# One more turn of queries in the wait for the fold: a recurrent attention's forward loop on one Trainium2 core

## The chip, the cores and the metric

The kernel runs on one core of a Trainium2 chip, as one launch. The metric is the device time of that launch in microseconds (us). The engines are named as the profile names them: PE (TensorE's matmuls), PEld (its weight loads), DVE (VectorE), ACT (ScalarE), POOL (GpSimd) and SP (SyncE, which only issues transfers here). PE reads its operands from SBUF and writes to PSUM; DVE and ACT copy from PSUM to SBUF.

## The reference, cut to what matters

The program is one training step, forward and all gradients, of `x + s * g`: `g` is a gated feed-forward of the normalised input, `s` a recurrent attention over it. Only the recurrence matters here:

```python
for s in range(n_seg):                       # 64 segments of 32 tokens
    h = concatenate([mem, xs], axis=1)       # 8 memory rows and 32 tokens, 640 wide
    q, k, v = h @ Wq, h @ Wk, h @ Wv         # 32 heads of 128
    p = softmax(where(mask, q k^T * scale, -1e9))
    o = (p v) @ Wo
    mem = o[:, :M]                           # the next segment's memory
    outs.append(o[:, M:])
```

Only the 8 memory rows pass from one segment to the next, so a segment's memory rows are a chain through all 64 steps. The tokens' rows of a segment hang on the chain, but nothing of the chain hangs on them.

## The kernel before, in words

`phase3_Afwd` (L389) runs the forward recurrence. Its loop, in `recurrence` (L555), has 64 steps. A step `t` consists of two things woven into each other:

- `chain(t, gap)` (L598): the memory rows of segment `t`. With `packed_half` (L301) it projects hx (8 memory rows and 24 riding rows, turned) by Wk, Wq and Wv, each in two halves, into the PSUM banks bA and bB. DVE copies the halves of Wk and Wq to SBUF (`k.copy`, L90), ACT those of Wv; `packed_sel` (L311) picks out the memory rows. Then come scores (L647), a soft-max over DVE and ACT, the weighted sum (L682), and the output projection `packed_out` (L317, matmuls at L325). `fold_add` (L330) then folds that projection's two halves: ACT copies one half (fup, L334), DVE adds the other in two parts (fsum, L336). `fold_turn` (L346, L352) turns the sum on PE, and DVE writes it into the next step's hx (L699). Nothing of step t + 1 can be projected before that.
- The batched work of the tokens of earlier segments, three segments together in a "tile" `tl`, in units of four heads `(tl, qd)`. A tile has eight units, three in two of the steps and two in the third (SPL, L890), from step 3 on (`batch`). `FILL` (L918) puts their parts into the gaps of the chain, which are named W0, W1, V0, W2, G1 to G6.

The parts of a unit that the change and the steps of the prediction touch:

- `ld("q", ...)` (L747): SP loads a unit's queries, memory rows (L245 or L754) and token rows (L265), into `xq`, of which there are two buffers. The first and second unit of step t + 1 are loaded in gap G1 of step t, the third in G5.
- `turn_q` (L760): four matmuls against the identity (L765) turn the four heads' queries into a PSUM tile qpt, and one ACT copy (L767) brings it to one of three SBUF tiles xqT. In before it is called for a step's first unit in G5 of the step ahead, for the second in W0, for the third in G1. `scores` (L769), which reads them, comes in G2.
- `turn_p` (L835): the same for the soft-max's results (L840, DVE copy L841); they come from POOL's `norm` (L832).
- `pv` (L882; matmuls L860 and L863), in W0 and W1, and `kprep` (L738, matmuls L743), in G4 and, for a third unit, in W0.
- The PSUM tiles of all of these come from one pool of five (tag "x"): a new one waits until an earlier one is read out.

At the end of some gaps PE gets filling matmuls without a use (L914, L915): the identity times 512 columns of Wq, into bank bA or bB. `WARM` (L564) says how many: one in G2, two in G3, two in G5. G5 lies between `fold_add` and `fold_turn`.

The order of all instructions is that of the program as written: `in_order` (L273, called at L1065) holds every engine to it. Semaphores alone decide when each one starts.

Of the kernel before, what the change touches and what calls it, by code (L numbers as in the profile page):

```python
# [554 lines left out]
def recurrence(k, W0, W4, Wv, Wk_, Wq, Wo, own, ps, banks):  # L555
    nc, tc = k.nc, k.tc
    D, DC, S, H, HD, T = k.D, k.DC, k.S, k.H, k.HD, k.T
    with tc.tile_pool(name="achain", bufs=1) as ch, \
# [5 lines left out]
        WARM = dict(G2=1, G3=2, G5=2)  # L564

        def ride_ld(t):
            x0 = k.NB0 + 24 * t
            b, sub = t // 4, t % 4
            if sub == 0 and x0 < S:
                w = min(96, S - x0)  # L570
                rt = ch.tile([P, DC, 96], BF16, name="ride", tag="ride")
                turned_load(k, rt[:, :, 0:w], k.XN[x0:x0 + w, :])
                rides[b] = (rt, w)
# [133 lines left out]
        def w_alloc(nm_):  # L707
            if nm_ == "o":
                WT["o"] = W0.tile([P, DC, HD], BF16, name="WoT", tag="w0")
                src = k.A_Wo.rearrange("h e d -> (h e) d")  # L710
                wfetch.extend([(WT["o"][:, :, r:r + 256], src[r:r + 256, :]) for r in range(0, HD, 256)])
            elif nm_ == "q":
                WT["q"] = W0.tile([P, H, D], BF16, name="WqT", tag="w1")
            else:
                WT["k"] = W4.tile([P, H, D], BF16, name="WkT", tag="w2")
                src = k.A_Wk.rearrange("d h e -> d (h e)")
                wfetch.extend([(WT["k"][:, h0:h0 + 2, :], src[:, h0 * P:(h0 + 2) * P]) for h0 in range(0, H, 2)])

        def w_ld(n):
            for _ in range(n):  # L720
                if wfetch:
                    turned_load(k, *wfetch.pop(0))
# [9 lines left out]
        def ld_k(tl, qd):  # L732
            c0 = qd * 512
            kr = fl.tile([96, 512], BF16, name="kr", tag="kr", bufs=2)
            k.load_x(kr, 0, k.x_src(tl, "k", c0, c0 + 512), nc.sync)
            uu["kr", tl, qd] = kr

        def kprep(tl, qd, eng='s'):  # L738
            ns, nm, nx, n = k.geo(tl)
            kr = uu.pop(("kr", tl, qd))  # L740
            pt = ps.tile([P, 4, nx], BF16, name="kpt", tag="x", bufs=5)
            for j in range(4):
                nc.tensor.transpose(pt[:, j, :], kr[0:nx, j * P:(j + 1) * P], k.ident[0:nx, 0:nx])  # L743
            dst = kTs[tl % 2][:, qd * 4:qd * 4 + 4, 0:n].rearrange("p h (s c) -> p h s c", c=40)[:, :, :, 8:40]
            k.copy(dst, pt[:].rearrange("p h (s c) -> p h s c", c=32), eng=eng)

        def ld(w, tl, qd, eng=nc.sync):  # L747
            nm = k.geo(tl)[1]
            c0 = qd * 512
            r = fl.tile([120, 512], BF16, name=f"x{w}", tag=f"x{w}", bufs=2 if w == "q" else 3)  # L750
            if qd >= (5 if w == "q" else 2):
                ns, nm, nx, n = k.geo(tl)
                g0 = 512 * (qd % 2)
                eng.dma_start(r[nx:n], k.QVM[3 * tl:3 * tl + ns, :, qd // 2, "qv".index(w), g0:g0 + 512].rearrange("t r c -> (t r) c"))  # L754
            else:
                k.load_m(r, tl, w, c0, c0 + 512, eng)
            k.load_x(r, 0, k.x_src(tl, w, c0, c0 + 512), eng)
            uu[w, tl, qd] = r
# [45 lines left out]
        def soft_exp(tl, qd, j0=0, j1=4):  # L804
            n = k.geo(tl)[3]
            sp, (nmx, Z), Pb = uu["s", tl, qd], uu["m", tl, qd], xPs[qd % 3]
            if nmx is None:
                nc.scalar.activation(Pb[0:n, :, 0:n], sp[0:n], ACT.Exp, scale=k.scale)
                uu["zs", tl, qd] = Pb
            else:  # L810
                for j in range(j0, j1):
                    nc.scalar.activation(Pb[0:n, j, 0:n], sp[0:n, j, :], ACT.Exp, bias=nmx[0:n, j:j + 1], scale=k.scale,  # L812
                                         accum_out=Z[0:n, j:j + 1])
            if j1 == 4:
                uu["z", tl, qd] = Z
                uu.pop(("s", tl, qd))
                uu.pop(("m", tl, qd))
# [25 lines left out]
        def oride_ld(t):  # L843
            if 0 <= t - k.OT0 < k.NO:
                r = ch.tile([P, H, 24], BF16, name="oride", tag="oride")
                nc.sync.dma_start(r[:], k.OTX[t - k.OT0])
                uu["o", t] = r

        def oride(t):
            if 0 <= t - k.OT0 < k.NO:  # L850
                nc.gpsimd.tensor_copy(oTm[:, :, 8:32], uu.pop(("o", t))[:])
# [15 lines left out]
        def pv_turned(tl, qd, eng='s', qo=nc.scalar):  # L867
            v, pt, po = uu["pv", tl, qd]
            if pt is not None:
                ot = fl.tile([P, 4, 4, 24], BF16, name="xoT", tag="xoT", bufs=2)  # L870
                k.copy(ot[:].rearrange("p c h t -> p h c t"), pt[:].rearrange("p h (c t) -> p h c t", t=24), eng=eng)
                qo.dma_start(k.OTX[4 * tl:4 * tl + 4, :, 4 * qd:4 * qd + 4, :].rearrange("c p h t -> p c (h t)"),
                             ot[:].rearrange("p c h t -> p c (h t)"))
# [17 lines left out]
        batch = {}  # L891
# [5 lines left out]
        def gap_of(t):  # L897
            def at(f, tt, i):
                b = batch.get(tt, ())
                if i < len(b):  # L900
                    f(*b[i])

            def gap(g):
                FILL(g, t, at, kbatch)
                if t == T - 1:
                    if g == "G1":
                        w_alloc("o")
                        ld("q", *tail[0])
                        ld("q", *tail[1])
                    if g == "G2":  # L910
                        next(work)
                    if g in ("G2", "G4"):
                        w_ld(2)
                for i in range(WARM.get(g, 0)):  # L914
                    nc.tensor.matmul((bA if g == "G4" else bB)[:], k.ident[:], Wq[:, 0, 0:512], start=True, stop=True)  # L915
            return gap

        def FILL(g, t, at, kbatch):  # L918
            kb = kbatch.get(t, ())
            if g == "W0":  # L920
                oride_ld(t)
                at(pv, t - 1, 0)
                at(turn_q, t, 1)
                for u in kbatch.get(t - 1, ())[2:]:
                    kprep(*u)
            elif g == "W1":
                at(pv_mm, t - 1, 1)
                at(pv_turned, t - 1, 1)
                at(turn_p, t - 1, 2)
                at(lambda a, b: ld("v", a, b), t - 1, 2)  # L930
            elif g == "V0":
                at(pv_rows, t - 1, 1)
            elif g == "W2":
                ride_ld(t + 1)
                for u in kb[0:2]:
                    ld_k(*u)
            elif g == "G1":
                oride(t)
                at(pv_mm, t - 1, 2)
                at(turn_q, t, 2)  # L940
                for i in range(2):
                    at(lambda a, b: ld("q", a, b), t + 1, i)
            elif g == "G2":
                at(lambda a, b: pv_turned(a, b, qo=nc.gpsimd), t - 1, 2)
                at(pv_rows, t - 1, 2)
                for i in range(3):
                    at(scores, t, i)
                at(soft_max, t, 0)
                for i in range(2):
                    at(lambda a, b: ld("v", a, b), t, i)  # L950
            elif g == "G3":
                at(lambda a, b: soft_exp(a, b, 0, 2), t, 0)
                at(soft_max, t, 1)
            elif g == "G4":
                at(lambda a, b: soft_exp(a, b, 2, 4), t, 0)
                at(lambda a, b: soft_max(a, b, True), t, 2)
                at(norm, t, 0)
                at(soft_sub, t, 2)
                for u in kb[0:2]:
                    kprep(*u, 'v')  # L960
                for u in kb[2:]:
                    ld_k(*u)
                at(soft_exp, t, 1)
                at(norm, t, 1)
                at(soft_exp, t, 2)
            elif g == "G5":
                at(turn_p, t, 0)
                at(turn_q, t + 1, 0)
                at(lambda a, b: ld("q", a, b), t + 1, 2)
            elif g == "G6":  # L970
                at(turn_p, t, 1)
                at(norm, t, 2)
# [56 lines left out]
        batch = {t: b for t, b in batch.items() if t < T}  # L1029
# [1262 lines left out]
```

## Time and profile before

| | us |
|---|---|
| Median of three runs | 4702.92 (4698.06 to 4706.8) |
| The profiled execution | 4684.61 |
| Its span, first to last instruction | 4682.7 |
| PE busy | 4466.5 (95%) |
| PEld busy | 2821.1 (60%) |
| DVE busy | 2244.7 (48%) |
| POOL busy | 2098.4 (45%) |
| ACT busy | 1587.4 (34%) |
| Mean granted clock of PE | 0.988 of full |
| L915, the fillers: 320 matmuls, one each | 0.379 |
| L765, turns of queries: 704 matmuls, one each (median) | 0.216 |
| L767, their ACT copies: 176, one each (median) | 0.558 |

The forward loop lies between about 369 and 1582 us of the span. Matmuls run into each other in PE's pipeline, and their ends are modelled, so the duration of one is longer than the distance to the next; costs of PE are better read from the starts. Weight loads (PEld) run beside matmuls. The releaser in brackets behind a row is what ended the idle time of its engine just before it.

### The profile page before, as it was taken

The page shows a single profiled execution, that of the slowest core. Times are in us where ns is not written, and L with a number is a line of the kernel's source. Part 1 is how long each engine was busy: PE and PEld are TensorE (multiplying, and loading weights), DVE is VectorE, ACT ScalarE, POOL GpSimd, SP SyncE. Part 2 cuts the span into 40 slices and gives each one's busy share as a digit, 9 for nine tenths or more (in the row PEclk, how much of TensorE's full clock was granted, in tenths as well). Part 3 has the DMA queues.
Part 4 walks back from the last instruction along what each step waited for, and adds up shares of the span by engine and source line. Part 5 has one row for each costly group of instructions (what it writes and reads, how often), then busy time and mean ns, then how long its engine had stood idle before and what let it go on. Part 6 is the DMA issues. An engine that isn't in the chain of part 4 may idle for free. (4 is left out here: it accounts for less than half of the span.)

```text
span 4682.7 us, 159785 instructions
## 1 busy us (share of the span) xinstructions
PE 4466.5 (95%) x64504; PEld 2821.1 (60%) x64504; DVE 2244.7 (48%) x7156; ACT 1587.4 (34%) x4360; POOL 2098.4 (45%) x3528
## 2 busy tenths in 40 slices
PE   8999999999999898999999998999999999999999
PEld 4544555555555555666666665676667666666675
DVE  8734666666666534555555553343224432311460
ACT  5432555555544433333333332232223322200000
POOL 6532555555555423455444444354335533311440
PEclk9999999999999998999999999999999999999999
DMA  8773566666655677777777775664345543579783
GB/s 269 236 252 119 175 178 178 179 179 179 180 168 167 167 181 230 211 225 207 215 211 209 208 209 154 144 163 132 110 116 158 147 129 107 170 223 207 159 181 100
DMA packets 976843, 834.77 MB, mean 178 GB/s; under 512 B 518890, under 2 KB 858286, under 8 KB 974144
## 3 DMA queue, kind: packets, MB, share of 16 engines
q1 hardware_dynamic: 763879, 547.92, 42.2%
q0 software_dynamic: 129952, 228.13, 16.4%
q10 hardware_dynamic: 82275, 48.52, 4.0%
q8 instruction: 509, 8.34, 0.8%
q14 instruction: 228, 1.87, 0.1%
HBM read 472.66 MB, written 310.33 MB: 167 GB/s over the span
## 5 line engine op out<-in xcount | busy, mean ns | idle before, releaser
L1667 PE MATMUL wg<-gr,hr 128*128 128x512 bf16 x2400 | 521.7, 379 | 0.0
L1648 PE MATMUL g<-land,ghacc 128*128 128x320 bf16 x3072 | 459.9, 300 | 0.8
L1667 PEld LDWEIGHTS <-hr 128*128 128x128 bf16 x2400 | 233.9, 98 | 278.9
L306 PEld LDWEIGHTS <-hx 128*32 128x32 bf16 x10240 | 246.8, 96 | 229.1 <-issue 14.6
L1648 PEld LDWEIGHTS <-ghacc 128*128 128x128 bf16 x3072 | 289.2, 98 | 104.2 <-ACT ghacc L92 2.2
L90 DVE CAST wgo<-wg 128x512 bf16<-128x512 f32 x72 | 49.8, 692 | 471.2 <-PE wg L1667 471.2
L90 DVE CAST stg<-bank 128x512 bf16<-128x512 f32 x256 | 177.1, 692 | 158.6 <-PE bank L306 154.5
L880 POOL DMA_DIRECT2D OR<-xv x163 | 89.8, 551 | 361.1 <-ACT xv L92 338.5
L1613 POOL DMA_DIRECT2D GSP<-grs x48 | 25.5, 542 | 473.1 <-ACT grs L1605 472.0
L92 ACT COPY ghacc<-t6g 128x768 bf16<-128x768 bf16 (+1 forms) x176 | 137.1, 779 | 293.8 <-PE t6g L1630 284.5
L1324 POOL DMA_DIRECT2D VTD<-gvT x176 | 129.4, 742 | 218.7 <-ACT gvT L1323 209.5
L325 PEld LDWEIGHTS <-gkv 128*8 128x8 bf16 x8192 | 177.6, 86 | 82.2 <-issue 4.1
L832 POOL TENSOR_TENSOR xP<-xP,xrz 120x480 bf16<-120x480 bf16 x163 | 161.1, 988 | 76.0 <-DVE xrz L831 46.6
L812 ACT ACTIVATE xP<-xsp,xnm 120x120 bf16<-120x120 f32 (+1 forms) x540 | 186.1, 372 | 26.0 <-DVE xnm L794 25.9
L1654 DVE TENSOR_TENSOR ghacc<-ghacc,g 128x320 f32<-128x320 f32 x192 | 93.6, 487 | 209.9 <-PE g L1648 209.9
L336 DVE TENSOR_TENSOR fsum<-bank,fup 64x160 bf16<-64x160 f32 x254 | 69.5, 311 | 258.5 <-ACT fup L334 255.2
L92 ACT CAST wgo<-wg 128x512 bf16<-128x512 f32 x48 | 28.1, 585 | 479.8 <-PE wg L1667 407.0
L1371 POOL DMA_DIRECT2D GXP<-gks x157 | 91.0, 580 | 189.5 <-ACT gks L1369 188.8
L325 PE MATMUL bank<-Wo,oTm 128*32 128x320 bf16 x4032 | 154.2, 307 | 18.4 <-DVE oTm L684 18.4
L325 PE MATMUL bank<-WkT,gkv 128*8 128x320 bf16 x4096 | 162.8, 299 | 4.2 <-issue 2.2
L325 PE MATMUL bank<-WvT,gkv 128*8 128x320 bf16 x4096 | 166.4, 305 | 0.5 <-DVE gkv L1197 0.5
L306 PE MATMUL bank<-Wq,hx 128*32 128x512 bf16 x2560 | 161.6, 381 | 0.0
(389 smaller groups left out, 10916.1 us busy)
## 6 DMA issues: line engine op xcount, KB each, us to landing
QVS<-stg SPq DMA_DIRECT2D x128, 256.0 KB
kT<-VTD SPq DMA_DIRECT2D x64, 320.0 KB
PR<-xP POOLq DMA_DIRECT2D x168, 120.0 KB, 3.1
VTD<-gvT POOLq DMA_DIRECT2D x168, 120.0 KB, 4.0
land<-DSR SPq DMA_DIRECT2D x168, 120.0 KB
land<-PR SPq DMA_DIRECT2D x168, 120.0 KB
OR<-xv POOLq DMA_DIRECT2D x163, 120.0 KB, 3.0
orr<-OR SPq DMA_DIRECT2D x14, 1280.0 KB
```

What stands on the lines that cost most here:

```text
L90: return nc.vector.tensor_copy(out, in_)
L92: return nc.scalar.copy(out, in_)
L306: k.nc.tensor.matmul(bank[32 * g:32 * g + 32, :], x[:, dc, :], W[:, dc, c0:c0 + 512], start=(dc == 0), stop=(dc == k.DC - 1), tile_positio ...
L325: k.nc.tensor.matmul(pm[p0:p0 + nq, 0:320], x[:, h, :], W[:, h, 320 * b:320 * b + 320], start=(first and i == 0), stop=(last and i == 15), ...
L812: nc.scalar.activation(Pb[0:n, j, 0:n], sp[0:n, j, :], ACT.Exp, bias=nmx[0:n, j:j + 1], scale=k.scale, accum_out=Z[0:n, j:j + 1])
L832: eng.tensor_tensor(Pb[0:n, :, 0:n], Pb[0:n, :, 0:n], bc_last(rz[0:n], n), ALU.mult)
L880: q.dma_start(k.OR[120 * tl:120 * tl + n, c0:c0 + 512], v[0:n])
L1324: nc.gpsimd.dma_start(k.VTD[tl][:, :, h0:h0 + 4, :], vTq[:])
L1371: (nc.sync if (tl, qd) in pro else nc.gpsimd).dma_start(k.GXP[tl, :, qd, 0:ns], ks[:].rearrange("p s i h m -> p s i (h m)"))
L1648: nc.tensor.matmul(pg[:], ring[:, i, j, r0:r0 + P], Ws[qd][i][:, j, 320 * h:320 * h + 320], start=(i == 0 and j == 0), stop=(i == 2 and j ...
L1654: nc.vector.tensor_tensor(a, a, pg[:], ALU.add)
L1667: nc.tensor.matmul(pw[:], hr[:, tl, dc * P:(dc + 1) * P], grs[i][:, tl, :], start=(tl == 0), stop=(tl == NF - 1))
```

## The change

`turn_q` of a step's second unit moves from gap W0 of its own step to gap G5 of the step ahead, right behind the first unit's; and G5 issues one filling matmul less in those steps whose next step has a second unit (steps 2 to 62).

```diff
@@ gap(g), in gap_of(t)
-                for i in range(WARM.get(g, 0)):
+                for i in range(WARM.get(g, 0) - (len(batch.get(t + 1, ())[1:2]) if g == "G5" else 0)):
                     nc.tensor.matmul((bA if g == "G4" else bB)[:], k.ident[:], Wq[:, 0, 0:512], start=True, stop=True)
@@ FILL(g, t, at, kbatch)
             if g == "W0":
                 oride_ld(t)
                 at(pv, t - 1, 0)
-                at(turn_q, t, 1)
                 for u in kbatch.get(t - 1, ())[2:]:
                     kprep(*u)
...
             elif g == "G5":
                 at(turn_p, t, 0)
                 at(turn_q, t + 1, 0)
+                at(turn_q, t + 1, 1)
                 at(lambda a, b: ld("q", a, b), t + 1, 2)
```

`at(f, t, i)` calls `f` for unit `i` of step `t`'s batch, if there is one.

## The prediction, made before the changed kernel was run

> **What bounds the kernel now.** First the share of busy time on the page: PE (matmuls) is busy for 95% of the span and no other engine reaches 50%. That is an average over stages, so next comes one step of the forward loop, cut at its waits, in the table by stretch. The step runs from one output projection to the next (888.80 to 907.47). Its columns are the stretch, its length, then busy time and instructions of PE, PEld (weight loads), DVE, ACT and POOL, the granted clock, the DMA share and GB/s.
>
> ```profile
> 888.80:890.65 1.85, 1.80 (x20) 1.09 (x17) 1.06 (x4) 0.98 (x2) 1.54 (x3) 1.00 0.85 269
> 890.65:893.68 3.03, 3.03 (x54) 1.59 (x52) 1.68 (x3) 0.32 (x1) 0.80 (x2) 1.00 0.64 206
> 893.68:899.55 5.87, 5.87 (x106) 2.70 (x104) 2.88 (x8) 2.76 (x6) 0.56 (x1) 1.00 0.53 151
> sum 18.67, PE 18.16 PEld 10.83 DVE 11.87 ACT 9.53 POOL 8.81; mean PE 3.03 PEld 1.80 DVE 1.98 ACT 1.59 POOL 1.47
> ```
>
> The second and third stretch are the projections of K, Q and V with what is put between them (gaps W0, W1): PE is busy in every hundredth, no other engine in half. What is taken from PE there shortens the step. The first stretch is the fold: ACT copies half of the projection out of PSUM, DVE adds, PE turns, DVE writes the next step's hx. PE looks busy there too, but with filling, so I read the order of work.
>
> ```profile
> 888.63 0.38 PE L840 MATMUL xpp<-ident,xP 120*128 120x120 bf16 x4
> 888.80 0.42 ACT L334 COPY fup<-bank 64x320 f32<-64x320 f32 x1 [0.68 <-PE bank L325]
> 888.85 0.37 PE L765 MATMUL qpt<-ident,xq 120*128 120x120 bf16 x4
> 889.06 0.60 PE L915 MATMUL bank<-Wq,ident 128*128 128x512 bf16 x2
> 889.26 0.55 DVE L336 TENSOR_TENSOR fsum<-bank,fup 64x160 bf16<-64x160 f32 x2 [0.85 <-ACT fup L334]
> 889.26 0.56 ACT L767 COPY xqT<-qpt 128x480 bf16<-128x480 bf16 x1
> 889.63 0.70 PEld L352 LDWEIGHTS <-fsum 64*128 64x128 bf16 x6 [0.46 <-DVE fsum L336]
> ```
>
> (Start, length, engine, line.) The fold's first weight load, at 889.63, is released by DVE's fsum, not by the filling before it. So G5 (P turn, Q turn, two fillers) is inside a wait.
>
> **The change part by part.** Call the moved turn Q1: turn_q of a step's second unit, four weight loads and four matmuls on PE and one ACT copy. It is made in steps 3 to 63, 61 times. The order of instructions of the two built kernels confirms that PE loses one filler (L915) and moves Q1 per step, and that Q1 comes after Q0 and before the one filler left.
>
> What leaves W0. The rows are where it stands now, and, for what is left, the same pair of neighbours in W1 and a step with a kprep behind it:
>
> ```profile
> 893.16 0.39 PE L863 MATMUL xpo<-xv,xPT 120*128 120x128 bf16 x4
> 893.38 0.37 PE L765 MATMUL qpt<-ident,xq 120*128 120x120 bf16 x4
> 893.68 1.26 PE L306 MATMUL bank<-Wq,hx 128*32 128x512 bf16 x20
> ...
> 896.55 0.39 PE L863 MATMUL xpo<-xv,xPT 120*128 120x128 bf16 x4
> 896.87 1.26 PE L306 MATMUL bank<-Wv,hx 128*32 128x512 bf16 x20
> ...
> 912.04 0.37 PE L765 MATMUL qpt<-ident,xq 120*128 120x120 bf16 x4
> 912.25 0.34 PE L743 MATMUL kpt<-ident,kr 96*128 96x96 bf16 x4
> ```
>
> Lengths overlap (matmuls are pipelined), so I use distances between starts. Without a kprep behind Q1 (21 steps, t a multiple of 3): xpo to Wq now takes 893.68 - 893.16 = 0.52; with Q1 gone xpo meets a projection as in W1, 896.87 - 896.55 = 0.32; saved 0.20. With a kprep (40 steps): 912.25 - 912.04 = 0.21 saved. Sum: 21 x 0.20 + 40 x 0.21 = 4.2 + 8.4 = 12.6 us. The bounds are 0, if it is not passed on, and 61 x 0.30 = 18.3 (Q1 to Wq counted whole).
>
> Is Wq ready 0.2 earlier? It needs bank A, copied by DVE (L90) from 892.02 to 892.71, 0.97 ahead of 893.68. The first K selection follows 1.2 later and needs DVE's second copy, 893.10 to 893.79: still 0.9 ahead. The copies behind wait for PE, not PE for them (in the loop DVE's stg waits 146.9 us in 201 cases for PE).
>
> What enters G5. Q1 for one filler: Q0, the same work, takes 889.06 - 888.85 = 0.21; a filler takes 0.60 - 0.38 = 0.22. So PE's fill keeps its length: it ends at about 889.06 + 2 x 0.22 = 889.50, while the fold goes at 889.63; cover 0.13. Were each weight load exposed at its 98 ns, Q1 would take 0.39: 0.17 over the filler, 0.04 past the cover, 61 x 0.04 = 2.4 us lost. I take 0, because the neighbour Q0 takes 0.21 in this very place.
>
> New waits of Q1, with the fold's turn queued behind it on PE and DVE's hx and all of the next step behind that: (a) its queries. Their last load is issued on SP at 884.28 and done issuing at 884.69; by the DMA semaphores in the trace such loads land 2.1 us after their issue (median), at least 2.0 ahead of the first filler in every step from 4 on. Cover 2 us. (b) a PSUM tile of the five: in the new order the one freed by the soft-max exponentials of unit 1 (three-unit steps) or by DVE's kprep copy. The exponentials of this step end at 888.13, 0.9 ahead of 889.06; in three-unit steps ACT has a further 0.62 us exponential after them, which itself ends 0.48 before the first filler. Cover 0.9 or more. Neither adds a wait.
>
> ACT: Q1's copy (0.56) moves from 894.92 to right behind Q0's, about 889.82 to 890.38. Ahead of it on ACT is the fold's fup; behind it nothing until 893.36, where ACT has idled 3.54. Cost 0; without that cover it would delay pv's copies by 0.56. In W1 ACT gets emptier, which PE does not wait for. The later PSUM users in W0 and W1 now take tiles freed by copies of G5, over 2 us old. Q1 issues no DMA, so SP and POOL are not passed; the third queries' load behind it on SP waits for Q0 alone.
>
> [...] Row first: the granted clock is 1.00 in every stretch above, G5 among them, in which transposes already stand, and the loop has it at 0.99. [...] By the row the price is 0. [...]
>
> Sum: -12.6 + 0. The profiled execution took 4684.6 (span 4682.7 and 1.9 around it), so it would become 4672.0. The median of the runs is 4702.9, 0.4% above it; the same 12.6 off it gives 4690.
>
> **The rivals.** (1) Nothing or little is passed on: something later in the step has its own pace, and PE, 0.2 earlier, waits there. Candidates are the two waits behind the projections (ACT's sTm, DVE's Pm). Against: both start from PE's own scores, and DVE, ACT and POOL have 6.8, 9.1 and 9.9 us free of 18.67; what is early at Wq stays early. For: POOL and SP come in bursts, and POOL's xP ends only 0.3 to 0.5 before the P turns. A half passed on gives 4697, none 4703.
> (2) Slower: Q1 stands before the fold and one of its inputs is late, so it stalls what the step's chain waits for. Any stall beyond 0.13 is paid whole, 61 times. It breaks even with the gain at 12.6 / 61 = 0.21 beyond the cover; a stall of 0.5 beyond it gives 61 x 0.5 - 12.6 = +18, 4721. It decides from queries landing over 2 us later than they do, or exponentials 0.9 later. Against it are those covers; for it, that a handful of steps of the loop are 0.3 to 1.5 us longer than their neighbours without a cause that I found, so single steps may be hit.
> [...]
> (4) The change does less than it says: Q1 was hidden in W0. The first fence speaks against it: PE has no idle time there.
>
> **How the numbers follow.** About 0.2% is what a measurement of this kernel can tell from no change: 9.4 us. Forecast 0.74: 4690, its own range 4684 to 4696, the odd stalls moving by 3 us or so either way. Rivals 1 and 4 together 0.18: 4695 to 4706. Rival 2 0.07, rival 3 0.01. Of the forecast's share about 0.70 lies beyond 9.4 us. So: faster 0.70, same 0.22, slower 0.08. The range 4683 to 4701 leaves out the slow cases, those with no gain at all, and little at the low end.
>
> **What would show it.** In the changed profile: the period of a step shorter by 0.20 to 0.21 (18.66, 19.24 and 19.04 us for t = 0, 1, 2 modulo 3 in the first two thirds of the loop); xpo to Wq 0.32 in W0; qpt twice in G5 at a distance of 0.21 and one L915; the time from ACT's fup to the fold's first weight load unchanged at 0.83, still released by fsum; clock 1.00. I am wrong in rival 2's way if the fold is released by PE's own order or qpt shows a wait for ACT or a DMA, and in rival 1's way if W0 is shorter but the idle time before L657 or L674 grows by as much.

## The result, and the profile after

| | before | after |
|---|---|---|
| Median, six runs each | 4700.49 us (4691.73 to 4712.89) | 4679.06 us (4674.76 to 4682.72) |
| Profiled execution, its span | 4684.61, 4682.7 | 4678.86, 4677.0 |
| Instructions on PE and on PEld, each | 64504 | 64443 |
| Forward loop, first to last write of hx (L699) | 1176.8 | 1166.8 |
| All the rest of the span | 3505.9 | 3510.2 |

The ratio is 0.9958, with an interval of 0.9945 to 0.9971: 20 us less (14 to 26). The direction was forecast, but not this size; the time lies 4 us under the range. The profiled executions differ by less, 5.7 us: that of before happened, by chance, to be 16 us under its own median.

The timeline of the changed kernel's G5 and W0 (the step with the same number as the one shown of before) shows both ends of the move.

```profile
888.36 0.42 ACT L334 COPY fup<-bank 64x320 f32<-64x320 f32 x1 [0.67 <-PE bank L325]
888.41 0.58 PE L765 MATMUL qpt<-ident,xq 120*128 120x120 bf16 x8
888.81 0.55 DVE L336 TENSOR_TENSOR fsum<-bank,fup 64x160 bf16<-64x160 f32 x2 [0.84 <-ACT fup L334]
888.82 1.02 ACT L767 COPY xqT<-qpt 128x480 bf16<-128x480 bf16 x2
888.83 0.38 PE L915 MATMUL bank<-Wq,ident 128*128 128x512 bf16 x1
889.18 0.70 PEld L352 LDWEIGHTS <-fsum 64*128 64x128 bf16 x6 [0.31 <-DVE fsum L336]
...
890.00 0.20 DVE L699 CAST hx<-bank 128x40 bf16<-128x40 f32 x1 [0.33 <-PE bank L352]
```

```profile
892.71 0.39 PE L863 MATMUL xpo<-xv,xPT 120*128 120x128 bf16 x4
893.03 1.26 PE L306 MATMUL bank<-Wq,hx 128*32 128x512 bf16 x20
```

Eight turns (x8) take 888.83 - 888.41 = 0.42, so each 0.21; the fold still starts 889.18 - 888.36 = 0.82 behind fup (0.83 before), released by fsum. In W0 xpo now meets Wq at a distance of 0.32 (0.52 before). The starts of L699 give the step: 18.45, 19.05 and 18.84 us for 18.66, 19.24 and 19.04, and 18.11, 18.49 and 18.50 in the last third for 18.32, 18.70 and 18.70. That is 0.19 to 0.21 in each kind, as forecast.

PE's waits further on did not grow: before L657 it was idle 16.7 us in all before and 16.6 after, before L674 53.9 and 53.3.

Not every step is typical. In steps 8 and 18 the changed kernel took 22.04 and 20.30 us, before 20.60 and 19.02. This is the table by stretch (length, then busy time and instructions of PE, PEld, DVE, ACT and POOL, granted clock, DMA share, GB/s) over the first projections of step 8, before and then after:

```profile
527.30:530.80 3.50, 3.50 (x72) 1.89 (x61) 2.05 (x4) 0.85 (x2) 2.07 (x3) 1.00 0.22 59
```

```profile
527.30:530.80 3.50, 3.50 (x36) 1.32 (x38) 1.84 (x4) 0.00 (x0) 2.52 (x4) 0.51 0.19 53
```

The clock column fell from 1.00 to 0.51, and 36 matmuls were done where 72 had been, though PE counts as busy for all 3.50 us in both. Ahead of it, in both kernels, PE had waited for POOL in G6, again before and then after:

```profile
526.43 0.22 PEld L840 LDWEIGHTS <-xP 120*128 120x128 bf16 x4 [1.63 <-POOL xP L832]
```

```profile
527.15 0.22 PEld L840 LDWEIGHTS <-xP 120*128 120x128 bf16 x4 [1.64 <-POOL xP L832]
```

So about the same idle time (1.63 and 1.64 us) was followed by half the clock in one kernel and not in the other. The expectations below call such a fall of the granted clock a closing of the clock gate.

### The profile page after: what moved, and what is told of

Read it like the earlier page. It is cut to its first block, busy times and chain, and to the rows that moved or that the text cites. A ratio compares the mean times of both kernels' runs of the same rounds, so it can differ in the third digit from the quotient of the medians.

```text
span 4677.0 us, 159650 instructions
## 1 busy us (share of the span) xinstructions
PE 4454.0 (95%) x64443; PEld 2818.5 (60%) x64443; DVE 2244.2 (48%) x7156; ACT 1588.7 (34%) x4360; POOL 2104.2 (45%) x3528
## 5 line engine op out<-in xcount | busy, mean ns | idle before, releaser
L245 POOL DMA_DIRECT2D land<-GOS x256 | 146.7, 579 | 36.5 <-issue 10.2
```

The lines of the kernel that those rows point to most:

```text
L245: eng.dma_start(d, src if src.shape[0] > 1 else src[0])
```

## The experiments

All ratios are to the kernel before, timed beside on the same chip. Four theories of the time beyond the forecast's 12.6 us run through the expectations. A: it is chance. B: the change itself brings some 20 us. C: it comes with the smaller number of instructions on PE. D: it comes with the smaller work of filling in G5.

What equal kernels give, and the change again:

**e0_same_again**: no edit. 

> The kernel before, unchanged, run as if it were a change. Theory A (the moved turn saves 12.6 us, what was measured beyond that is variation between executions, which is wider for the kernel before): ratio 1 within about 0.0015, which tells how far two equal kernels come out apart. Theory B (the change itself brings about 21 us): the same, ratio 1.

Measured: 1.0001 (0.9991 to 1.0011). Single runs of one kernel scatter by about 6 us (standard deviation), which is why an interval is some 5 us wide to each side.

**e1_change_again, e8_change_third, f3_change_fourth**: the changed kernel.

> The changed kernel again, unchanged. Theory A: 12.6 us less than before (ratio 0.9973), between 9 and 17. Theory B: 18 to 24 us less again (ratio about 0.9955).

> The changed kernel once more. Two comparisons gave 21 and 17 us less, three kernels with the same typical step (two fillers, a narrow one, none) 14, 10 and 13. Theory A (all of them are the moved turn's 12.6 and chance): 9 to 16 less. Theory B (the change as it stands has 5 us more than its variants, somewhere outside the typical step): 16 to 22 less.

> The change once more, for comparison on the same chip: 12.6 for the moved turn and 5 of surplus, 14 to 20 less.

Measured: 0.9964 (0.9950 to 0.9977), 0.9969 (0.9957 to 0.9981), 0.9965 (0.9952 to 0.9978); medians 4687.6, 4687.47 and 4690.93 us. With the first, four comparisons with a mean of 0.9964, 17 us. The forecast's 12.6 (0.9973) lies in each of the last three intervals and outside the first. In the four profiled executions the loop takes 1166.8, 1165.6, 1164.6 and 1170.9; in three kernels with nothing moved (before, e0, e7) 1176.8, 1177.5 and 1180.0. The means differ by 11.1. The rest of the span has a mean of 3518.5 in those four and 3518.4 in these three, so these executions show no gain outside the loop; but the single values reach from 3505.9 to 3526.5, and a few us could hide in that.

The two halves of the change apart:

**e2_one_filler_only, e9_one_filler_third**: before, with the reduced count of fillers and `at(turn_q, t, 1)` left in W0. (The same line of the gradient loop was edited alike, L1429; that loop fills in G4 alone, so nothing changes there.)

```diff
-                for i in range(WARM.get(g, 0)):
+                for i in range(WARM.get(g, 0) - (len(batch.get(t + 1, ())[1:2]) if g == "G5" else 0)):
```

> Only the filler is dropped in G5 of steps 2 to 62; the turn of the second unit's queries stays in W0. Theory A: no change, 0 +- 4 us, since fsum and not the filling releases the fold; its first weight load stays 0.83 us behind the start of fup. Theory B, if the surplus comes from the dropped filler: 6 to 10 us less.

> Only the filler dropped, nothing moved, once more. It was 6 us less (1 to 11), its narrow form 0. Theory A: 0 +- 4. Theory B, with the dropped filler as its cause: 4 to 8 less.

Measured: 0.9987 (0.9977 to 0.9997) and 0.9988 (0.9977 to 0.9999): 6 us less, with 0 just outside the intervals. The typical steps are those of before, 18.66, 19.25 and 19.04, so the loop does not show where the 6 us are. Theory A expected none.

**e3_two_fillers_kept**: the change, with `range(WARM.get(g, 0))` as before.

> Only the turn is moved from W0 to G5; both fillers stay. Theory A: PE's filling ends 0.21 us later, some 0.08 to 0.14 past the point where fsum is ready; 12.6 less 61 x 0.08 to 0.14 = 4 to 8 us less than before. Theory B, if the surplus comes from the move of the turn and not from the filler: 12 to 16 us less.

Measured: 0.9971 (0.9959 to 0.9983), 14 us less: more than theory A gave it. Its G5:

```profile
850.05 0.42 ACT L334 COPY fup<-bank 64x320 f32<-64x320 f32 x1 [0.22 <-PE bank L325]
850.10 0.58 PE L765 MATMUL qpt<-ident,xq 120*128 120x120 bf16 x8
850.52 0.60 PE L915 MATMUL bank<-Wq,ident 128*128 128x512 bf16 x2
851.05 0.52 PEld L352 LDWEIGHTS <-fsum 64*128 64x128 bf16 x6 [0.42 <-DVE fsum L336]
851.70 0.20 DVE L699 CAST hx<-bank 128x40 bf16<-128x40 f32 x1 [0.33 <-PE bank L352]
```

The fold's first weight load comes 1.00 behind fup instead of 0.82, but hx is written 851.70 - 850.05 = 1.65 behind it, as before (1.65) and after (1.64). The six loads take 0.52 here and 0.70 there: they start early and then wait for fsum's second half, or start late and run through. The steps are 18.45, 19.04 and 18.83.

**e10_three_fillers**: the change with `WARM = dict(G2=1, G3=2, G5=4)`, so three fillers behind the two turns.

> The turn moved, and three fillers in G5 in place of the change's one (four in the wait of step 0 and 1): PE's filling is 0.44 us longer than in the changed kernel. With two fillers the fold started 0.17 later but ended at the same time, being closed up behind the second half of fsum. If that was all of the cover, the third filler is paid whole: 61 x 0.22 = 13 us more than with two fillers, so no gain over the kernel before (-2 to +4), and steps of 18.66, 19.25 and 19.04. If filling before the fold costs nothing at all, 13 less as before.

Measured: 0.9987 (0.9977 to 0.9996), 6 us less than before, some 8 us more than with two fillers. In the typical steps it is as expected: 18.63, 19.22 and 19.01, 0.18 longer than with two; and its loop, 1176.8, is that of the kernel before. Its G5:

```profile
856.79 0.42 ACT L334 COPY fup<-bank 64x320 f32<-64x320 f32 x1 [0.21 <-PE bank L325]
857.21 0.37 PEld L915 LDWEIGHTS <-ident 128*128 128x128 bf16 x3
858.01 0.49 PEld L352 LDWEIGHTS <-fsum 64*128 64x128 bf16 x6 [0.42 <-DVE fsum L336]
858.62 0.20 DVE L699 CAST hx<-bank 128x40 bf16<-128x40 f32 x1 [0.51 <-PE bank L352]
```

hx comes 858.62 - 856.79 = 1.83 behind fup instead of 1.65. So the cover ends just behind the second filler.

**e11_turn_twice_in_W0**: before, with the turn's matmuls doubled where they stood.

```diff
-                at(turn_q, t, 1)
+                at(lambda a, b_: turn_q(a, b_, 2), t, 1)
...
-            for j in range(4):
+            for j in list(range(4)) * times:
```

> The kernel before, with the four matmuls of the second unit's turn made twice in W0 (the second time over the same PSUM tile; the result is the same). If PE alone paces W0 and what is put there is passed on whole, 61 x 0.21 = 12.8 us more than before (ratio 1.0027), each step longer by 0.21. If part of it is covered by a wait further on, less; if W0's price were the 20 us that the changed kernel seemed to save, 20 more.

Measured: 1.0032 (1.0020 to 1.0044), 15 us more; 12.8 lies inside. The typical steps are 18.87, 19.45 and 19.25: 0.21 longer each. In W0 the eight turns take 880.62 - 880.20 = 0.42:

```profile
879.98 0.39 PE L863 MATMUL xpo<-xv,xPT 120*128 120x128 bf16 x4
880.20 0.58 PE L765 MATMUL qpt<-ident,xq 120*128 120x120 bf16 x8
880.62 0.34 PE L743 MATMUL kpt<-ident,kr 96*128 96x96 bf16 x4
```

W0 is paced by PE alone, and its work is passed on whole.

How little filling is enough:

**e5_no_filler_in_wait**: the change, with `2 * len(...)` fillers fewer in G5.

> The change, and the other filler of G5 dropped too in steps 2 to 62. The typical step should stay at 18.45, 19.04 and 18.83 us by all theories, the fold being released by fsum. Theory C or D: another 5 us less, 21 to 24 less than before. Theory A (the filler's 5 us were chance): as the change, 12 to 17 less. If the clock gate closes for lack of filling, which it does in steps 8 and 18 of the changed kernel and not in the kernel before, more windows at half clock inside the loop, each worth about 1.6 us, and the gain falls.

Measured: 0.9973 (0.9963 to 0.9983), 13 us less, with the clock at half for 3.4 us in steps 8 and 18, as in the change, and nowhere else from step 4 on. Dropping this last filler brought nothing more; theories C and D had both expected that it would.

**e6_no_fillers_in_loop**: the change with `WARM = dict()`.

> The change, and all fillers of the loop dropped (one in G2, two in G3, the rest in G5; 259 more). Theory C or D, if what one filler costs holds for these: 259 x 5 / 61 = 21 us less again, 35 to 40 less than before, as long as the clock stays granted. Clock gate: without filling PE idles about 0.5 us in G2, 0.4 in G3 and 0.4 in G5 of each step; if that closes the gate in a third of the steps, 20 x 1.6 to 2 = 30 to 40 us more, and the gain is gone. Theory A: 12 to 17 less.

Measured: 1.0104 (1.0088 to 1.0120), 49 us more than before. The table by stretch over its loop, and then that of the change:

```profile
393.80:604.00 210.20, 188.31 (x3710) 115.90 (x3711) 125.49 (x351) 94.45 (x303) 97.91 (x156) 0.96 0.53 154
604.00:1002.00 398.00, 370.65 (x6922) 232.29 (x6919) 241.51 (x675) 196.78 (x628) 209.14 (x326) 0.93 0.59 170
1002.00:1614.80 612.80, 565.64 (x10835) 353.38 (x10833) 383.36 (x1080) 295.17 (x979) 329.20 (x513) 0.94 0.57 167
```

```profile
393.00:604.00 211.00, 198.91 (x3768) 117.60 (x3769) 126.47 (x354) 95.93 (x305) 99.28 (x158) 0.96 0.53 156
604.00:1002.00 398.00, 382.70 (x7458) 233.34 (x7457) 257.91 (x721) 210.73 (x679) 225.44 (x350) 1.00 0.61 181
1002.00:1559.80 557.80, 538.07 (x10485) 325.57 (x10485) 365.88 (x1033) 280.62 (x926) 312.17 (x486) 1.00 0.58 175
```

The clock column is the cause: 0.93 and 0.94 where it was 1.00. The trace has 37 windows of half clock from step 9 on, all but one of 3.4 us. The loop has 143.3 us of half clock, that of the change 20.5; the difference makes some 36 windows, so its 1221.0 - 1166.8 = 54 us more are about 1.5 us a window. All but the long one begin within a us of the start of the output projection, behind the waits that G2 and G3 used to fill. This is PE ahead of such a window, which begins at 640.4:

```profile
638.47 0.24 PE L674 MATMUL bank<-ident,Pm 128*40 128x128 bf16 x2 [0.19 <-DVE Pm L669]
639.12 0.59 PE L682 MATMUL bank<-PTm,vt 40*128 40x8 bf16 x32 [0.41 <-ACT PTm L676]
639.64 0.51 PE L743 MATMUL kpt<-ident,kr 96*128 96x96 bf16 x8
640.58 1.79 PE L325 MATMUL bank<-Wo,oTm 128*32 128x320 bf16 x24 [0.42 <-DVE oTm L684]
```

No idle time of PE from step 9 on is over 0.82 us.

Where the surplus comes from (the change's 17 less the 12.6, the lone filler's 6):

**e7_before_narrow_filler**: before, with G5's second filler at 8 of 512 columns. **e4_moved_narrow_filler, f4_moved_narrow_again**: the change, with that narrow filler in place of the dropped one. The edit is the same on both kernels (in e4 and f4 the count of fillers is again that of before):

```diff
-                    nc.tensor.matmul((bA if g == "G4" else bB)[:], k.ident[:], Wq[:, 0, 0:512], start=True, stop=True)
+                    w = 8 if g == "G5" and i == 1 and len(batch.get(t + 1, ())) > 1 else 512
+                    nc.tensor.matmul((bA if g == "G4" else bB)[:, 0:w], k.ident[:], Wq[:, 0, 0:w], start=True, stop=True)
```

> The kernel before with G5's second filler at 8 columns in place of 512, and nothing moved. Theory C (number of instructions): no change, 0 +- 4. Theory D (the filler's work): 4 to 6 us less, as when it was dropped. Theory A: 0 +- 4.

> The turn moved as in the change, but G5's second filler is kept at 8 columns in place of 512: as many instructions on PE as with two fillers, and about 0.2 us less work in each of the 61 waits. The dropped filler was worth some 5 us in two comparisons, though no typical step got shorter by it. Theory C (the number of PE's instructions: what they are fetched as, or where later code comes to lie): as with two whole fillers, 11 to 14 us less than before. Theory D (the filler's work itself): as the change, 16 to 18 less.

> The turn moved and G5's second filler at 8 columns, once more (it was 10 less). Theory C: 10 to 14 less. Theory D: 15 to 20 less, if the first time was chance.

Measured: 1.0001 (0.9991 to 1.0011); 0.9979 (0.9968 to 0.9989) and 0.9978 (0.9966 to 0.9990). Against theory D: taking the filler's work away and leaving its instructions brought nothing. That is what theory C expected.

**f1_change_same_count**: the change, and in G2 one filler of 8 columns more.

```diff
+                if g == "G2" and len(batch.get(t + 1, ())) > 1:
+                    nc.tensor.matmul(bB[:, 0:8], k.ident[:], Wq[:, 0, 0:8], start=True, stop=True)
```

> The change, and in G2 of steps 2 to 62 one more filler of 8 columns behind the one that is there, in a wait with 0.5 us to spare: PE has as many instructions again as before the change, G5 is filled as in the change. Theory C (the surplus of some 5 us comes with the smaller number of PE instructions): 10 to 14 us less than before. Theory D (it comes from how G5 is filled): 15 to 20 less, as the change.

Measured: 0.9970 (0.9957 to 0.9983), 14 us less, at the edge of theory C's range and just outside D's; with this interval it tells nothing apart.

**f2_one_filler_less_in_G3**: before, with the count reduced in G3 instead of G5.

```diff
-                for i in range(WARM.get(g, 0)):
+                for i in range(WARM.get(g, 0) - (len(batch.get(t + 1, ())[1:2]) if g == "G3" else 0)):
```

> The kernel before with one of G3's two fillers dropped in steps 2 to 62, nothing moved: as many PE instructions fewer as when one of G5's is dropped. Theory C: 3 to 8 less. Theory D: 0 +- 4, or some more time if the clock gate closes for it.

Measured: 1.0006 (0.9994 to 1.0017). By itself that would speak against theory C. But the run is not clean: in its profiled execution the clock fell to half five times between steps 3 and 61 (17, 23, 26, 32 and 35); these steps took 1.6 to 4.0 us more than the 19.04 of a typical one of their kind, and the loop took 1187.2, 9 us more than in before, e0 and e7. That the whole is only 3 us slower leaves room for C's 5. It decides nothing.

## Why the prediction was right in its mechanism and wrong in its size

- **"Sum: 21 x 0.20 + 40 x 0.21 = 4.2 + 8.4 = 12.6 us."** Right where it was counted: every kind of typical step lost 0.19 to 0.21, and doubling the same work made each 0.21 longer and cost 15 us (9 to 21).
- **"Is Wq ready 0.2 earlier?" and passed on whole.** Right: the idle time before L657 and L674 did not grow; the whole step shortened by what W0 lost. Rivals 1 and 4 are out, and so is rival 2: the fold is still released by fsum. One reading on the way was wrong, without harm: in the stretch of 3.03 us another engine is busy for more than half, DVE with 1.68 (55%). Its copies end 0.9 ahead of their use all the same.
- **"Cover 0.13" in G5, and "any stall beyond 0.13 is paid whole".** The price of 0 was right, the cover too small. I measured it at the fold's first weight load, but hx waits for the last, and that waits for fsum's second half. The first load may start some 0.2 later still: in e3 it is 0.17 later and hx is unmoved, in e10 0.39 later and 0.18 of that is paid.
- **The granted clock, "by the row the price is 0".** This is a step that failed too, though toward a longer time, not a shorter one. The row, 1.00, was one of a typical step; the price falls in steps 8 and 18, where PE waits for POOL anyway (in after PEld's first load of that wait comes after 1.64 us idle in step 8, 1.76 in step 18). In each of the two the clock fell to half in three of the four profiled executions of the change, never in before and e0, at about 1.5 to 1.6 us a window: some 2 us together, enough for the 1.5 between 12.6 and the loop's 11.1 (f3 has a window of twice the length in step 46 besides). Over all profiled executions but e6's, step 8 has a window in 7 of the 10 with the turn moved and in 1 of the 7 with it in W0, step 18 in 6 and in 1. So they are more frequent with the turn moved. What brings them about is not shown, and that it is a lack of filling, as e5's expectation has it, is not shown either: e3, which keeps both fillers beside the moved turn, has both windows, but e2 and e7, where nothing is moved and a filler is dropped or narrowed, have one each. Rival 3, to which the prediction gives 0.01, was a stretch of half clock in every step. That was an estimate of mine, and no run of the change shows it: in after the clock is at half for 20.5 us of the loop's 1166.8, from step 4 on in steps 8 and 18 alone.
- **"Forecast 4690, its own range 4684 to 4696, the odd stalls moving by 3 us or so".** This step set the range, and it failed: besides the 12.6 it allowed for the odd stalls of the loop alone, and took the scatter of the measurement itself for too small. The forecast was 11 us too high. 2.4 of these are the place that it was counted from, a median of three runs (4702.92) that came out as 4700.49 in six. The other 9 are gain beyond the 12.6. The repeats gave 17, 15 and 16 us where the first comparison gave 20, so a part of the 9 was chance; some 3 to 4 came again, and whether these are real, and where they would come from, stays open. Four medians of the same changed kernel are 4679.1, 4687.6, 4687.5 and 4690.9, over 12 us. Three of them lie in the range, the first under it.
- **What stays open.** The change gave 17 us in the mean of four, its loop 11 in the profiles. Outside the loop no gain is to be seen: without e6, the rest of the span has a mean of 3518.8 in the seven profiled executions with the turn in W0, and of 3522.1 in the ten with it moved. Dropping the filler alone gave 6 twice, without a shorter step. Theory D (the filler's work) is contradicted by the narrow fillers (0, and 10 less twice where it said 15 to 20). Theory C (fewer instructions) agrees with these, but not with e5, nor with e10: that kernel issues 64571 weight loads on PE where before issues 64504, its typical steps are only 0.03 shorter, and yet it measured 6 us less. The one further test of C, f2, decides nothing, and how fewer instructions would save time no run shows. All nine comparisons with the turn moved and at most two fillers behind it (0, 1, 2 or a narrow one) lie between 0.9958 and 0.9979, with a mean of 0.9970, 14 us; with intervals of 5 to 6 us to each side they may all be one value near the forecast's 12.6 with chance on top (theory A). I cannot tell that from a real surplus of about 4 us.

## What to carry to other kernels

Work that an engine does without a pause in one stage can be moved into a wait of the same engine in another, and the price of its old place can be read from the distance between the starts of its neighbours (here 0.20 to 0.21 us read, 0.19 to 0.21 found). The size of a wait's cover is read at the last instruction that the chain needs, not at the first one that is released (in e3 the first came 0.17 us later and hx did not). And a filler can be replaced by work in one wait, but with no filler left in the loop (e6) the granted clock past its first steps was 0.93 and 0.94 where the change has 1.00, and the kernel took 49 us more than before: test them one by one, and look at the rare steps where PE waits anyway, not only at the typical one.

## What the runs showed of the hardware that I had not expected

In e6 the clock fell to half in 37 windows from step 9 on, and no idle time of PE there is over 0.82 us, a few of them in a step; in step 8 of before 1.63 us were followed by a clock of 1.00. The distances from one window's start to the next in e6 are all whole multiples of 3.413 us, the length of a window: 20.48 (six times it) in 26 of 36 cases, else 37.55, 58.03 and others. In the clock records of before and after the distances are whole multiples of it too, and so is the length of each stretch at half clock but the last, which the end of the record cuts off. Seventeen steps of e6 in a row (12 to 28) have one window each, 14.4 to 15.8 us behind hx; the windows themselves stretch these steps to 20.40 in the mean, so near to 20.48 that they stay almost in phase. What brings the clock down no run here shows. And a busy PE tells nothing of the clock: the 3.50 us of step 8 are fully busy at 1.00 and at 0.51.
